# Chunked attention in TensorE's 64x64 tiles, in one section per eight feed-forward units

## Chip, cores, metric

One core of a Trainium2 chip runs the whole kernel. The metric is device time in microseconds (us), the median of several executions. The engines are TensorE (PE, matmuls; PEld is its weight load), VectorE (DVE), ScalarE (ACT), GpSimd (POOL) and SyncE (SP), which issues nearly all DMAs.

## The reference

The first half is a linear attention with decay, over 4 batches, 8 heads, 768 positions and 64 channels; the second is a feed-forward layer on the result, as 3072 tokens of 512 channels.

```python
for b in range(nb):                       # blocks of 64 positions
    qb, kb, vb = (q[:, :, sl], k[:, :, sl], v[:, :, sl])
    intra = np.einsum('bhic,bhjc->bhij', qb, kb) * Dmask[None]
    intra = np.einsum('bhij,bhjd->bhid', intra, vb)
    inter = np.einsum('bhid,bhde->bhie', qb * lam_pow[None], kv_state)
    out[:, :, sl] = intra + inter
    kv_state = lam_block * kv_state + np.einsum('bhsd,bhse->bhde', kb_dec, vb)
...
h = x @ w_in                              # 512 -> 2048
g = h * (1.0 / (1.0 + np.exp(-h)))        # SiLU
return g @ w_out                          # 2048 -> 512
```

## The kernel before

**Tiling.** The 3072 tokens are 24 chunks of 128 positions, six to a batch. A head has 64 channels, so two heads form a pair and the eight heads four pairs (NP). GROUPS (L17) collects chunks into groups of 256 or 384 tokens for the feed-forward layer. All matmul inputs are bf16, all sums fp32.

**Preparation.** The decay is put into q and k: `prep` (L367) multiplies a chunk's q by a table that grows with the position and its k by one that falls, on POOL, to qb and kb. `dma_t` (L382) has two DMA transposes on SP's queue turn them into qt and kn (channels on partitions). `vcast` (L374) rounds v to bf16 on ACT. `next_prep` (L685) does this for the next chunk and issues the loads of a later one.

**Attention of a chunk, from the seventh (c >= 6) on.** TensorE is used whole, as 128x128, so a pair's two heads have to be kept apart by zeros. For that DVE spreads kn into ktbd (`move_k`, L408, 64x512) and v into vpad (`spread_v`, L394, 64x256): block-diagonal buffers whose other halves stay zero. Then come
- the scores (`pe_s`, L484): eight matmuls into two banks sp, four of 128 columns and four of 64, and the causal mask on DVE (`masked`, L494) to ss;
- the state (`pe_d`, L456): four matmuls into kv_ps, accumulated over a batch's chunks in PSUM, and the two diagonal halves copied by DVE into kvbd (`copy_kv`, L468); a batch's last chunk has none;
- the output (`pe_o`, L505): four matmuls of qt with kvbd (not in a batch's first chunk), four of 128 and four of 64 columns with ss, into one bank op, which ACT copies into xt, the feed-forward input (L530).

**Feed-forward.** An "up" unit computes hidden channels of a group: for 256 tokens `ffn1_two` (L553) two blocks of 128 channels in eight matmuls of 256 columns, for 384 tokens `ffn1` (L559) one block in four matmuls of 384. ACT applies Silu to each bank h_ps into g. A "down" unit (`ffn2`, L587) is four of the sixteen matmuls (512 columns) of 128 tokens into a bank o_ps; after the fourth unit DVE copies the bank to ob, and `tick` (L579) has SP store it two units later. The last 128 tokens are split in three (`ffn2_last`, L602).

**PSUM.** Eight banks: att (3), h (2), o (2), kv (1).

**What sets the order.** Each engine runs its queue in the order in which the program issues instructions. Chunks 0 to 3 follow a list written out by hand (ORDER, L25); their scores and outputs are already in 64x64 tiles (`op_s`, L295, and `op_o`, L311). Chunks 4 and 5 are written out below it (L714 to L743). From then on `stretch` (L778) merges lists of units by place: the ups of group g, the attention pieces of group g+1, and the downs of group g-1, evenly over the stretch. A piece is s (scores), d (state) or o (output) of a chunk; the first thing in `piece` (L746) is to prepare chunks up to c+3.

Of the kernel before, what the change touches and what calls it, by code (L numbers as in the profile page):

```python
# [16 lines left out]
GROUPS = [256, 256, 256, 256, 256, 384, 384, 384, 384, 256]  # L17
# [21 lines left out]
def kernel(  # L39
# [73 lines left out]
    for i in range(NKV):  # L113
        vpad.append(const.tile([128, NP, 4, D], BF16, name=f"vpad{i}"))
        ktbd.append(const.tile([128, NP, 2, BLK], BF16, name=f"ktbd{i}"))
        kvbd.append(const.tile([128, NP, BLK], BF16, name=f"kvbd{i}"))
# [73 lines left out]
    mask2 = const.tile([128, BLK], F32)  # L190
    for j in range(2):
        nc.gpsimd.tensor_copy(mask2[64 * j:64 * j + 64, :], mask[0:64, :])

    vhalf = [t.rearrange("s p x d -> s p (x d)").rearrange("s p (h j d) -> s p h j d", h=2, j=2) for t in vpad]
    khalf = [t.rearrange("d p j s -> d p (j s)").rearrange("d p (h j s) -> d p h j s", h=2, j=2) for t in ktbd]

    def clear_halves(*bufs):  # L200
        for i in bufs:
            nc.gpsimd.memset(ktbd[i], 0.0)
            nc.gpsimd.memset(vpad[i], 0.0)

    NBUF = {"att": 3, "h": 2, "o": 2, "kv": 1}
# [71 lines left out]
    def op_t(src, name):  # L277
        def run(c, a, tag):
            tp = psum.tile([128, 2, 2, BLK], BF16, name=name, tag=tag, bufs=NBUF[tag], padded_shape=[128, 4, 2, BLK])
            for r in range(2):  # L280
                for p in range(2):
                    nc.tensor.transpose(tp[:, p, r, :], src[c][:, a, r, 2 * p:2 * p + 2, :], ident)
            cell[name, c, a] = tp
        return run
# [10 lines left out]
    def op_s(c, a, *tags):  # L295
        sps = [psum.tile([128, 2, 2, 2, 64], F32, name="sp", tag=t, bufs=NBUF[t]) for t in tags]
# [14 lines left out]
    def op_o(c, a, *tags):  # L311
        for x, t in enumerate(tags):
            op_[c + x, a] = psum.tile([128, 2, 2, 64], F32, name="op", tag=t, bufs=NBUF[t], padded_shape=[128, NP, 2, 64])
# [47 lines left out]
    def prep_k(c, e="P"):  # L361
        kb = nat.tile([128, NP, 2, D], BF16, tag="kb")
        VG[e].tensor_tensor(kb, rawk.pop(c).rearrange("s (p j) d -> s p j d", j=2), decay(lam_bwd, c % NB),  # L363
                                op=AL.mult)
        natb[c] = (None, kb, vpad[c % NKV] if c < NPAD else nat.tile([128, NP, 2, D], BF16, name="vb", tag="vb", bufs=2))

    def prep(c):  # L367
        qb = nat.tile([128, NP, 2, D], BF16, tag="qb")
        nc.gpsimd.tensor_tensor(qb, rawq.pop(c).rearrange("s (p j) d -> s p j d", j=2), decay(lam_fwd, c % NB),  # L369
                                op=AL.mult)  # L370
        prep_k(c)
        natb[c] = (qb,) + natb[c][1:]

    def vcast(c, e="A"):  # L374
        if c in vraw and c >= NPAD:
            vb = natb[c][2]
            move(e, vb, vraw.pop(c).rearrange("s (p j) d -> s p j d", j=2))
            vnew.add(c)
# [3 lines left out]
    def dma_t(c):  # L382
# [5 lines left out]
        tr[c] = (qt, khalf[c % NKV])  # L388
        knat[c] = kn

    knat = {}
    vnew = set()

    def spread_v(c):  # L394
        if c in vnew:
            vnew.discard(c)
            vb, vh = natb[c][2], vhalf[c % NKV]
            for j in range(2):
                for h in range(2):
                    nc.vector.tensor_copy(vh[64 * j:64 * j + 64, :, h, j, :], vb[64 * h:64 * h + 64, :, j, :])  # L400

    def spread_k(c):
        if c in knat:
            kn = knat.pop(c)
            for j in range(2):
                move_k("D", c, j, kn)

    def move_k(e, c, j, t):  # L408

        rows = slice(64 * j, 64 * j + 64)  # L410
        if c < NPAD:
            move(e, ktbd[c % NKV][rows, :, j, :], t[rows, :, :])
        else:
            move(e, khalf[c % NKV][rows, :, :, j, :], t[rows, :, :].rearrange("d p (h s) -> d p h s", h=2))
# [3 lines left out]
    def pe_tq(c, tag):  # L418
        qb = qpairs.pop(c)
        tp = psum.tile([128, 2, NP, BLK], BF16, name="tq", tag=tag, bufs=NBUF[tag])  # L420
# [5 lines left out]
    def copy_qt(c, tp, e="A"):  # L426
# [4 lines left out]
        tr[c] = (qt, ktbd[c % NKV] if c < NPAD else khalf[c % NKV])  # L431

    def pe_tk(c, tag):
        kb = natb[c][1]
        tp = psum.tile([128, NP, BLK], BF16, name="tk", tag=tag, bufs=NBUF[tag], padded_shape=[128, 2 * NP, BLK])
# [7 lines left out]
    def st_t(c):  # L443
        qb, kb, vb = natb[c]
        tp = psum.tile([128, 2, NP, BLK], BF16, name="tp", tag="att", bufs=3)
        for p in range(NP):
            nc.tensor.transpose(tp[:, 0, p, :], qb[:, p, :, :], ident)
        for p in range(NP):
            nc.tensor.transpose(tp[:, 1, p, :], kb[:, p, :, :], ident)
        qt = nat.tile([128, NP, BLK], BF16, tag="qt")  # L450
        nc.vector.tensor_copy(qt, tp[:, 0, :, :])
        for j in range(2):
            move_k("D", c, j, tp[:, 1, :, :])
        tr[c] = (qt, khalf[c % NKV])

    def pe_d(c):  # L456
# [4 lines left out]
        if blk == 0:  # L461
            kvps[c // NB] = psum.tile([128, NP, BLK], F32, name="kv_ps", tag="kv", bufs=1)
        kv = kvps[c // NB]
        for p in range(NP):
            nc.tensor.matmul(kv[:, p, :], lhsT=kb[:, p, :, :], rhs=vb[:, p, 0:4:3, :] if c < NPAD else vb[:, p, :, :],  # L465
                             start=(blk == 0 and p == 0), stop=True, skip_group_check=True)
# [17 lines left out]
    def pe_s(c, j, tag="att"):  # L484

        qt, kt = tr[c]
        a = 0 if c < NPAD else 64 * j
        sp = psum.tile([128, NP, BLK - a], F32, name="sp", tag=tag, bufs=NBUF[tag], padded_shape=[128, NP, BLK])
        for p in range(NP):
            lhsT = kt[:, p, j, :] if c < NPAD else kt[:, p, j, :, :]  # L490
            nc.tensor.matmul(sp[:, p, :], lhsT=lhsT, rhs=qt[:, p, a:], start=True, stop=True)  # L491
        return sp

    def masked(sp, e="D", m=None):  # L494
        n = sp.shape[-1]
        ss = work.tile([128, 4, n], BF16, name="ss", tag="ss", padded_shape=[128, 4, BLK])
        m = mask if m is None else m
        VG[e].tensor_tensor(ss, sp, m[:, None, :n].to_broadcast([128, 4, n]), op=AL.mult)  # L498
        return ss

    def st_s(c):
        spread_k(c)
        st[c] = [masked(pe_s(c, j), m=mask if c < NPAD else mask2) for j in range(2)]

    def pe_o(c, tag="att"):  # L505
        blk = c % NB
# [3 lines left out]
        g, off = group_of[c]  # L510
        if off == 0:
            xt[g] = xpool.tile([128, KO_IN, GROUPS[g]], BF16, name="xt", tag="xt", padded_shape=[128, KO_IN, 512])
        op = psum.tile([128, NP, BLK], F32, name="op", tag=tag, bufs=NBUF[tag])
        terms = [(kvb[c][:, p, :], qt[:, p, :], op[:, p, :]) for p in range(NP)] if blk > 0 else []
        for j in range(2):
            if c < NPAD:
                terms += [(vb[:, p, 2 * j:2 * j + 2, :], res[j][:, p, :], op[:, p, :]) for p in range(NP)]
            else:
                terms += [(vhalf[c % NKV][:, p, j, :, :], res[j][:, p, :], op[:, p, 64 * j:]) for p in range(NP)]

# [3 lines left out]
        return op  # L524

    def st_o(c):
        spread_v(c)
        op = pe_o(c)
        g, off = group_of[c]
        nc.scalar.activation(xt[g][:, :, off * BLK:(off + 1) * BLK], op, AF.Copy)  # L530
# [6 lines left out]
    def ffn1_open(g, i, tag="h"):  # L537
        hps[g, i] = psum.tile([128, 512], F32, name="h_ps", tag=tag, bufs=2)
# [20 lines left out]
    def ffn1(g, m, part=None, tag="h", kos=range(KO_IN)):  # L559
        n = GROUPS[g]  # L560
        a, z = (0, n) if part is None else (part * n // 2, (part + 1) * n // 2)
        if (g, m) not in hps:
            hps[g, m] = psum.tile([128, 512], F32, name="h_ps", tag=tag, bufs=2)
        hp = hps[g, m]
        tick()
        for ko in kos:
            nc.tensor.matmul(hp[:, a:z], lhsT=w_in_bf[:, ko, m * 128:(m + 1) * 128], rhs=xt[g][:, ko, a:z],  # L567
                             start=(ko == 0 and a == 0), stop=(ko == KO_IN - 1), skip_group_check=True)
        if z == n and kos[-1] == KO_IN - 1:
            gg = gpool.tile([128, n], BF16, name="g", tag="g", padded_shape=[128, 512])  # L570
            nc.scalar.activation(gg, hp[:, :n], AF.Silu)  # L571
            gt[g, m] = gg

# [13 lines left out]
    def ffn2(g, mt, kos, tag="o"):  # L587
        tick()
        if kos[0] == 0:
            ops[g, mt] = psum.tile([128, DM], F32, name="o_ps", tag=tag, bufs=2)  # L590
# [11 lines left out]
    def ffn2_last(g, mt):  # L602

        r0 = gstart[g] + mt * BLK
        for i, (a, z, tag) in enumerate([(0, 256, "o"), (256, 384, "h"), (384, 512, "h")]):
            o = psum.tile([128, 512], F32, name="o_part", tag=tag, bufs=2)
# [21 lines left out]
    def op_u(g, b, h, *tags):  # L628
# [9 lines left out]
        for m, tag in zip(ms, tags):  # L638
            hps["m", m] = psum.tile([128, 512], F32, name="h_ps", tag=tag, bufs=2)
# [42 lines left out]
    fns = {"t": st_t, "d": st_d, "s": st_s, "o": st_o}  # L682
# [23 lines left out]
    for i in range(NKV):  # L706
# [35 lines left out]
    clear_halves(0, 1)  # L742
# [3 lines left out]
    def piece(c, kind):  # L746
        while state["prepped"] <= min(c + 3, NCHUNK - 1):
            next_prep()
        fns[kind](c)
        if kind == "s":  # L750
# [74 lines left out]
```

## Time and profile before

| what | value |
|---|---|
| time of three runs | 213.63, 214.12, 214.44 us; median 214.12 |
| span of the profiled execution, first to last instruction | 211.4 us |
| between this span and the median | 2.7 us |
| granted TensorE clock | 1.00 throughout |
| o_ps matmuls, 128x512 (L593) | 368, busy 91.7 us |
| h_ps matmuls, 128x384 (L567) and 128x256 (L544) | 256 and 288, busy 50.6 and 35.9 us |
| scores (L491), outputs (L522), state (L465) | 160, 228, 64 matmuls |
| Silu of 512 columns on ACT (L549) | 596 ns |
| copy of o_ps to ob on DVE (L597) | 691 ns |
| last matmul ends at | 208.7 us |

The profile is one execution; its span leaves out what lies before the first and after the last instruction, so the table sets it beside the median of the timed runs. In the lists of groups, a line gives source line, engine, operation, names and shapes, count, then busy time, mean ns of one, and the engine's idle time before them with what ended it. The timeline gives start, duration and operation, equal neighbours merged ("x8"). A matmul's duration holds its latency, and the next one starts before it ends; so the time that matmuls take is read from the distance of their starts.

### The profile page before, as it was taken

To read this page: it belongs to the slowest core of one execution; us is meant where nothing else is said; L and a number is where in the kernel's file an instruction comes from. 1 tells how busy PE (TensorE), PEld (TensorE's weight loads), DVE (VectorE), ACT (ScalarE), POOL (GpSimd) and SP (SyncE) were. 2 spreads that over 40 slices of the span, in tenths; PEclk is the share of its full clock that TensorE was granted. 3 is DMA by queue.
4 is the path that set the end of the run, shared out by engine and by line. 5 is a ranking of instruction groups with operands and counts; after the bars stand their busy time and mean duration, and the time that the engine had idled before them with its cause. 6 is when DMAs were issued, how large, how long until landed. Compare 5 with 4: busy or idle time off the path is not lost.

```text
span 211.4 us, 4349 instructions
## 1 busy us (share of the span) xinstructions
PE 204.5 (97%) x1698; PEld 127.5 (60%) x1698; DVE 116.3 (55%) x266; ACT 96.4 (46%) x183; POOL 54.1 (26%) x66
## 2 busy tenths in 40 slices
PE   7899999998999999999999999999999999999994
PEld 2467444566857877765665665556665565466654
DVE  3897458586287897563994686355552351110121
ACT  3686762514724664545454544445534344323210
POOL 6360004463933433341343333330000000000000
PEclk9999999999999999999999999999999999999999
DMA  4999999998979898999998999996111011011112
GB/s 118 337 368 393 394 399 284 287 228 186 269 203 208 168 248 212 201 204 143 229 204 176 233 247 197 225 239 139 50 50 54 0 50 54 0 50 50 53 50 99
DMA packets 95573, 38.57 MB, mean 182 GB/s; under 512 B 80960, under 2 KB 88512, under 8 KB 95552
## 3 DMA queue, kind: packets, MB, share of 16 engines
q1 hardware_dynamic: 92288, 37.50, 69.7%
q10 hardware_dynamic: 3264, 0.79, 1.7%
q8 instruction: 13, 0.21, 0.4%
q14 instruction: 8, 0.07, 0.1%
HBM read 27.27 MB, written 6.29 MB: 159 GB/s over the span
## 4 chain that ended last, share of the span: by engine, by line
PE 75%; DMA 13%; POOL 4%; SPq 3%; ACT 1%; issue 1%; ACTq 1%; DVE 0%; POOLq 0%
PE o_ps L593 32%; PE h_ps L567 18%; DMA qf<-in_q_dram 8%; PE h_ps L544 8%; PE h_ps L644 5%; PE op L522 4%; PE sp L491 3%; DMA kn<-kb 2%; DMA pair<-in_k_dram 2%; SPq L237 2%; POOL qb L369 2%; PE o_part L608 2%; POOL kb L363 2%; PE kv_ps L465 1%; PE kv_ps L343 1%
## 5 line engine op out<-in xcount | busy, mean ns | idle before, releaser
L593 PE MATMUL o_ps<-w_out_bf,g 128*128 128x512 bf16 x368 | 91.7, 379 | 0.0
L593 PEld LDWEIGHTS <-g 128*128 128x128 bf16 x368 | 34.9, 98 | 31.0
L571 ACT ACTIVATE g<-h_ps 128x384 bf16<-128x384 f32 x64 | 31.4, 490 | 47.3 <-PE h_ps L567 46.8
L567 PE MATMUL h_ps<-xt,w_in_bf 128*128 128x384 bf16 x256 | 50.6, 326 | 0.0
L597 DVE COPY ob<-o_ps 128x512 f32<-128x512 f32 x23 | 15.9, 691 | 42.2 <-PE o_ps L593 42.1
L544 PE MATMUL h_ps<-xt,w_in_bf 128*128 128x256 bf16 x288 | 35.9, 273 | 0.9 <-ACT g L549 0.9
L369 POOL TENSOR_TENSOR qb<-qf,lam_fwd 128x512 bf16<-128x512 f32 x18 | 18.8, 1045 | 60.6 <-DMA qf<-in_q_dram 60.6
L567 PEld LDWEIGHTS <-w_in_bf 128*128 128x128 bf16 x256 | 23.7, 98 | 17.2
L549 ACT ACTIVATE g<-h_ps 128x512 bf16<-128x512 f32 x36 | 21.1, 596 | 24.6 <-PE h_ps L544 24.3
L544 PEld LDWEIGHTS <-w_in_bf 128*128 128x128 bf16 x288 | 27.2, 98 | 6.5 <-issue 1.0
L498 DVE TENSOR_TENSOR ss<-sp,mask 128x512 bf16<-128x512 f32 (+1 forms) x40 | 21.0, 566 | 16.7 <-PE sp L491 16.3
L400 DVE COPY vpad<-vb 64x256 bf16<-64x256 bf16 x72 | 23.6, 328 | 2.4 <-ACT vb L184 0.9
L363 POOL TENSOR_TENSOR kb<-kf,lam_bwd 128x512 bf16<-128x512 f32 x20 | 21.7, 1088 | 2.3 <-DMA kf<-in_k_dram 2.1
L188 DVE CAST kvbd<-kv_ps 64x256 bf16<-64x256 f32 x34 | 14.3, 420 | 8.7 <-PE kv_ps L465 8.3
L530 ACT ACTIVATE xt<-op 128x512 bf16<-128x512 f32 x20 | 11.9, 597 | 15.1 <-PE op L522 14.5
L188 DVE COPY ktbd<-kn 64x512 bf16<-64x512 bf16 x36 | 14.5, 402 | 6.5 <-DMA kn<-kb 6.1
L491 PEld LDWEIGHTS <-ktbd 128*128 128x128 bf16 x160 | 9.4, 98 | 4.3 <-DVE ktbd L188 0.9
L184 ACT ACTIVATE vb<-vf 128x512 bf16<-128x512 f32 x18 | 11.2, 622 | 1.7 <-issue 1.7
L491 PE MATMUL sp<-qt,ktbd 128*128 128x128 bf16 (+1 forms) x160 | 10.3, 207 | 0.6 <-DVE ktbd L188 0.6
L644 PE MATMUL h_ps<-xt,w_in_bf 128*128 128x512 bf16 x48 | 10.5, 379 | 0.0
L522 PE MATMUL op<-ss,vpad 128*128 128x128 bf16 (+1 forms) x160 | 10.3, 207 | 0.0
L522 PEld LDWEIGHTS <-vpad 128*128 128x128 bf16 x160 | 8.9, 98 | 0.7
(84 smaller groups left out, 129.9 us busy)
## 6 DMA issues: line engine op xcount, KB each, us to landing
out_dram<-ob SPq DMA_DIRECT2D x23, 256.0 KB, 3.1
kf<-in_k_dram SPq DMA_DIRECT2D x19, 256.0 KB, 3.9
vf<-in_v_dram SPq DMA_DIRECT2D x19, 256.0 KB, 4.3
qf<-in_q_dram SPq DMA_DIRECT2D x17, 256.0 KB, 3.2
pair<-in_moe_w_out_dram SPq DMA_DIRECT2D x8, 512.0 KB, 7.7
pair<-in_moe_w_in_dram SPq DMA_DIRECT2D x6, 512.0 KB, 7.6
pair<-in_k_dram SPq DMA_DIRECT2D x4, 256.0 KB, 4.5
pair<-in_q_dram SPq DMA_DIRECT2D x4, 256.0 KB, 4.6
```

Source lines behind the costliest of these rows:

```text
L188: nc.vector.tensor_copy(dst, src)
L363: VG[e].tensor_tensor(kb, rawk.pop(c).rearrange("s (p j) d -> s p j d", j=2), decay(lam_bwd, c % NB), op=AL.mult)
L369: nc.gpsimd.tensor_tensor(qb, rawq.pop(c).rearrange("s (p j) d -> s p j d", j=2), decay(lam_fwd, c % NB), op=AL.mult)
L400: nc.vector.tensor_copy(vh[64 * j:64 * j + 64, :, h, j, :], vb[64 * h:64 * h + 64, :, j, :])
L491: nc.tensor.matmul(sp[:, p, :], lhsT=lhsT, rhs=qt[:, p, a:], start=True, stop=True)
L522: nc.tensor.matmul(dst, lhsT=lhsT, rhs=rhs, start=(i == 0), stop=(i >= len(terms) - NP), skip_group_check=True)
L544: nc.tensor.matmul(hps[g, i][:, a:a + 256], lhsT=w_in_bf[:, ko, m * 128:(m + 1) * 128], rhs=xt[g][:, ko, :], start=(ko == 0 and u == 0), s ...
L549: nc.scalar.activation(gg.rearrange("p u n -> p (u n)"), hps[g, i], AF.Silu)
L567: nc.tensor.matmul(hp[:, a:z], lhsT=w_in_bf[:, ko, m * 128:(m + 1) * 128], rhs=xt[g][:, ko, a:z], start=(ko == 0 and a == 0), stop=(ko == ...
L571: nc.scalar.activation(gg, hp[:, :n], AF.Silu)
L593: nc.tensor.matmul(o, lhsT=gt[g, ko][:, mt * BLK:(mt + 1) * BLK], rhs=w_out_bf[:, ko, :], start=(ko == 0), stop=(ko == KO_OUT - 1))
L644: nc.tensor.matmul(hps["m", m], lhsT=w_in_bf[:, ko, m * 128:(m + 1) * 128], rhs=xall[0][:, :, ko, :], start=(ko == 0), stop=(ko == KO_IN - 1))
```

## The change

1. **All groups have 256 tokens** (twelve); `ffn1` goes, every up is `ffn1_two`.
2. **No spreading.** From chunk 6 on ktbd and vpad are not filled; two instead of four of each exist, and the four POOL clears (`clear_halves`) go. Matmuls read kn, vb and kvs directly, one head at a time, as 64x64 tiles.
3. **`section(co, cs)`** issues output and state of chunk co and the scores of chunk cs together. It makes a list of matmuls for each of the four tiles (row half r of the inputs, column half x of the result) and merges the lists by an assumed time: 32 ns for 64 columns, 56 for others, always the tile that can begin first. Two row tiles may not write one bank at once. So for each such bank (kv and the two halves of op) one row tile leads; the other's first matmul is preceded by a `nop` that waits for the leader's last matmul (a turn), and the planner places it LAG = 220 ns behind that one's stream. A section has 56 matmuls where co is inside a batch, 48 for a batch's first chunk, 40 for its last, 24 for chunk 23; one more section, of scores alone (chunk 6), has 16.
4. **Behind the matmuls** DVE masks the scores in four products (64x256 twice, 128x256 twice), op is in two banks (two pairs each) and goes to xt in two copies of 128x256, on DVE in the first section of a group and on ACT in the second, and DVE copies the state once (128x256) to kvs.
5. **PSUM.** `bank("o")` takes the o banks in turn; a section takes three att banks and the o bank that the next `ffn2` will open.
6. **Order.** Per group: six ups, a section, two ups, six downs, a section, two downs; the downs are those of the same group. `vcast` stands behind the first and third down.
7. **POOL.** From chunk 6 on each multiplication is split in two, of 384 and 128 elements; the first swaps the two heads of its three pairs (a reversed read).

```diff
-GROUPS = [256, 256, 256, 256, 256, 384, 384, 384, 384, 256]
+GROUPS = [256] * 12
...
+    def bank(tag):
+        if tag != "o":
+            return {"tag": tag, "bufs": NBUF[tag]}
+        otag[0] = 1 - otag[0]
+        return {"tag": f"o{otag[0]}", "bufs": 1}
...
+        nc.gpsimd.tensor_tensor(dst[:, :3], src[:, :3, ::-1, :], by[:, :3, ::-1, :], op=AL.mult)
+        nc.gpsimd.tensor_tensor(dst[:, 3:], src[:, 3:], by[:, 3:], op=AL.mult)
...
+    at = [(1, 0), (1, 0), (1, 0), (0, 1)]
+    LAG = 220
+
+    def section(co=None, cs=None, e="A"):
...
+            ops = [psum.tile([128, 2, BLK], F32, name="op", tag=t, bufs=n, padded_shape=[128, NP, BLK])
+                   for t, n in (("att", 3), (f"o{1 - otag[0]}", 1))]
...
+            sps = [psum.tile([128, NP, BLK], F32, name="sp", tag="att", bufs=3) for j in range(2)]
+
+        def out(r, i):
+            first = {0, 1} if r == i else set()
+            for p in (2 * i, 2 * i + 1):
+                for j in range(2):
+                    x = at[p][j]
+                    add(r, x, i, vb[half[r], p, x, :], res[j][half[r], p, 64 * r:], ops[i][half[x], p % 2, 64 * r:], x in first)
+                    first.discard(x)
+                if blk:
+                    x = at[p][r]
+                    add(r, x, i, kvb[co][half[r], p, :], qt[half[r], p, :], ops[i][half[x], p % 2, :])
+
+        def state(r):
+            if blk < NB - 1:
+                for p in range(NP):
+                    for j in range(2):
+                        add(r, j, "kv", kb[half[r], p, j, :], vb[half[r], p, at[p][j], :], kv[half[j], p, :],
+                            blk == 0 and r == 1 and p == 0)
+
+        def scores(r):
+            if cs is not None:
+                for p in range(NP):
+                    for h in range(2):
+                        add(r, h, "s", kt[half[r], p, half[h]], qs[half[r], p, 64 * h:], sps[r][half[h], p, 64 * h:], True)
+
+        if co is not None:
+            out(0, 0)
+        scores(0)
+        if co is not None:
+            state(0), out(0, 1), state(1), out(1, 1)
+        scores(1)
+        if co is not None:
+            out(1, 0)
+
+        leads = {"kv": 1, 0: 0, 1: 1}
...
+        while any(jobs.values()):
+            k = min((k for k in jobs if jobs[k]), key=lambda k: (begin(k), k))
+            t = begin(k)
+            key, n, lhsT, rhs, dst, start = jobs[k].pop(0)
+            if leads.get(key, k[0]) != k[0] and key in last:
+                turn = nc.tensor.nop()
+                tc.add_manual_dep(turn.ins, last.pop(key).ins.name,
...
+            ins = nc.tensor.matmul(dst, lhsT=lhsT, rhs=rhs, start=start, stop=True, skip_group_check=True)
+            free[k] = t + (32 if n == 64 else 56)
+            if leads.get(key) == k[0]:
+                done[key], last[key] = max(free[k], done.get(key, 0)), ins
...
+            for rows, cols in ((half[0], half[0]), (slice(0, 128), half[1])):
+                m = mask[rows, cols]
+                for ss, sp in zip(st[cs], sps):
+                    nc.vector.tensor_tensor(ss[rows, :, cols], sp[rows, :, cols],
+                                            m[:, None, :].to_broadcast([m.shape[0], NP, 64]), op=AL.mult)
+        if co is not None:
+            x = new_xt(co)
+            for i, op in enumerate(ops):
+                move(e, x[:, 2 * i:2 * i + 2, :], op)
+            if blk < NB - 1:
+                kvs = nat.tile([128, NP, D], BF16, name="kvs", tag="kvs", bufs=2)
+                nc.vector.tensor_copy(kvs, kv)
+                kvb[co + 1] = kvs
...
-    clear_halves(0, 1)
     down0(3, 1)
...
+    def piece(co, cs, e="A"):
+        while state["prepped"] <= min(cs + 2, NCHUNK - 1):
+            next_prep()
+        section(co, cs if cs < NCHUNK else None, e)
...
+    for g in range(2, len(GROUPS) - 1):
+        c = 2 * g + 2
+        for i in range(8):
+            if g == 2 and i == 2:
+                vcast(6)
+                piece(None, 6)
+            if g == 2 and i == 4:
+                next_prep(2)
+            if i == 6:
+                piece(c, c + 1, "D")
+            ffn1_two(g, i)
+        for i, unit in enumerate(downs(g)):
+            if i == 1:
+                vcast(c + 1)
+            if i == 3 and c + 2 < NCHUNK:
+                vcast(c + 2)
+            if i == 6:
+                piece(c + 1, c + 2)
+            ffn2(*unit)
```

## The prediction

> **What bounds the kernel now.** I read the page first (busy shares, then the 40 slices), then the chain of work that ended last, then the waits, then TensorE's timeline.
>
> ```profile
> PE 204.5 (97%) x1698; PEld 127.5 (60%) x1698; DVE 116.3 (55%) x266; ACT 96.4 (46%) x183; POOL 54.1 (26%) x66
> ...
> PE   7899999998999999999999999999999999999994
> ...
> PE 75%; DMA 13%; POOL 4%; SPq 3%; ACT 1%; issue 1%; ACTq 1%; DVE 0%; POOLq 0%
> ```
>
> TensorE (PE) is busy in every slice from 10 us on, and the chain is 75% PE. No other engine is over 55%, so what DVE and POOL lose or gain counts only where PE has to wait for it. The DMA part of the chain lies at 66 to 99 us and ends in small PE waits; I price them below. So time follows the length of PE's stream, matmul by matmul, plus its waits. The timeline prices the stream (start in us, duration, operation; the distance of starts is the price, because matmuls overlap):
>
> ```profile
> 61.26 0.50 PE L491 MATMUL sp<-qt,ktbd 128*128 128x128 bf16 x8
> 61.60 1.03 PE L593 MATMUL o_ps<-w_out_bf,g 128*128 128x512 bf16 x4
> 62.47 0.39 PE L465 MATMUL kv_ps<-vb,kb 128*128 128x128 bf16 x4
> 62.69 1.03 PE L593 MATMUL o_ps<-w_out_bf,g 128*128 128x512 bf16 x4
> 63.55 0.39 PE L522 MATMUL op<-qt,kvbd 128*128 128x128 bf16 x4
> 63.78 0.50 PE L522 MATMUL op<-ss,vpad 128*128 128x128 bf16 x8
> 64.12 1.89 PE L593 MATMUL o_ps<-w_out_bf,g 128*128 128x512 bf16 x8
> ```
>
> Four kv_ps matmuls take 62.69-62.47 = 0.22 us, so 56 ns for 128 columns; the eight sp matmuls (four of 128, four of 64 columns) take 0.34, so 29 ns for 64 columns; o_ps takes 0.865 per four. A chunk's attention is 0.34+0.22+0.23+0.34 = 1.13 us of PE, and nothing but PE's order hides it.
>
> **Removed.** Chunks 6 to 23 issue 264 matmuls of 128 and 144 of 64 columns: 264 x 56 + 144 x 29 ns = 19.0 us (in the trace their starts add up to 18.9). DVE loses the copies into vpad (72, 23.6 us) and ktbd (36, 14.5 us), POOL the four clears: worth nothing by themselves, DVE is covered by PE. But two PE waits for ktbd go with them, and a third for ACT:
>
> ```profile
> 48.91 1.91 PE L544 MATMUL h_ps<-xt,w_in_bf 128*128 128x256 bf16 x16
> 51.67 4.53 PE L544 MATMUL h_ps<-xt,w_in_bf 128*128 128x256 bf16 x40 [0.85 <-ACT g L549]
> ...
> 98.35 1.03 PE L593 MATMUL o_ps<-w_out_bf,g 128*128 128x512 bf16 x4
> 99.82 0.51 PE L491 MATMUL sp<-qt,ktbd 128*128 128x128 bf16 x8 [0.44 <-DVE ktbd L188]
> ```
>
> Sixteen ups at 108 ns end at 50.64, the next starts at 51.67: 1.03 us. Likewise 99.82 - 99.21 = 0.61, and 0.34 at 71.68. The first wait (ACT is issuing three loads) is filled by chunk 6's scores, which the change puts there. The other two come from transposes that arrive late while chunks are taken every 5.3 us; afterwards one is taken every 7.8 us (eight ups, eight downs and two sections, 13.9 + 1.8 us, per two chunks), and loads and transposes run at 5.3 to 5.9 us a chunk here. I take all three: -2.0 us; at worst none.
>
> **Moved at no price.** Ups in 384 columns cost 0.65 us per four, so 163 ns for 384 against 108 for 256: the same per column (41.7 against 41.6 us for those tokens). Downs keep their 368 matmuls. Downs behind their own ups need the last Silu 2.6 us (three downs units) after the last up; it takes 0.6. Eight ups in a row were run at 51.67 without a gap, so ACT's 0.60 per 0.87 us keeps up. Of the copies into xt, those of the second chunk of a group are ACT's: 2 x 0.46 us behind the section, with two downs units (1.73 us) before the ups that read them: hidden with 0.7 to spare. POOL gets two multiplications for one; at 1.05 us per 512 elements its 2.2 us per 7.8 us are far from the bound even if the reversed read doubled them. The transposes, loads and stores on SP's queue are the same in number and order per chunk, and each chunk has more time.
>
> **Added: 19 sections.** The built order has 936 matmuls in 64x64 tiles, 408 of 128 and 528 of 64 columns. The kernel already does this in its first chunks:
>
> ```profile
> 12.33 0.40 PE L282 MATMUL tq<-ident,qb 128*128 128x128 bf16 x4
> 12.56 0.28 PE L318 MATMUL op<-qtp,kvbd 128*128 128x128 bf16 x2
> 12.77 0.42 PE L323 MATMUL op<-ss,vp 64*64 64x128 bf16 x16
> 13.12 0.40 PE L282 MATMUL tk<-ident,kp 128*128 128x128 bf16 x4
> 13.44 0.42 PE L301 MATMUL sp<-qtp,ktp 64*64 64x128 bf16 x16
> ```
>
> Sixteen tile matmuls take 0.35 us, not 16 x 56 = 0.90: four run at once. In the single records four start within 10 ns, and each round of four comes 56 ns after the last one.
> - Stream: (408 x 56 + 528 x 29)/4 ns = **9.5 us** if the four tiles are evenly filled.
> - Mode switches: the first round starts 149 ns after the last L318, not 56, and takes 80, not 56; from the start of the last round to the next L282 it is 159, not 56, and then 66, not 56. That is 93 + 24 + 103 + 10 ns, 0.23 us a visit; 19 x 0.23 = **4.4 us**.
> - Turns: 51 times the second row tile of a bank waits for the first one's last matmul (three per section with output, two without state). No such wait binds in this trace. A 128-column matmul ends 219 ns after its start, 163 after its stream; a semaphore of another engine releases PE within about 50 ns (ACT g to L544 at 51.67). From below 0: the order puts other tiles' work in front, by an assumed 220 ns. From above the whole 163+50+28 (a weight load) = 0.24 each, 12 us. Walking the built order of a full section (56 matmuls) with these prices I get 0.67 us from first to last where even filling gives 0.57: 0.10 x 18 = **1.9 us**, near the lower end, because the 220 ns is close to 0.24.
> - Supply: 56 pairs of load and matmul in under 0.7 us is denser than anything here. From below nothing; from above, 22 pairs were issued within 0.6 us of a late release at 10.98, so at most 27 ns a pair, 25 us for 936, 14 more than stream and turns. The nearest rows, blocks of 16 pairs, show no shortage, so I take 0.
>
> A 64x64 tile's weights load in 28 ns in the single records (second load of a tile after the first), just under the 29 ns of a 64-column matmul, so I count no extra for it.
>
> The Trainium skill speaks against this point: "TensorEngine Tiling (Array Packing)", Restrictions and Gotchas, says that column tiling excludes the fast weight load, and "TensorE: Matmul & The Clock Gate", LDWEIGHTS, gives a load as its columns over 1.2 GHz. By that an estimate of 53 ns per load would set the pace of the 64-column matmuls, 528 x 24/4 ns = 3.2 us more, about 214.8 in all.
>
> **The new wait.** In the section before the last two ups, both halves of op go to DVE, behind the four mask products. The second half's bank is the one that the group's first down takes, and PE's queue stops there: all later matmuls stand behind that first down. The rows:
>
> ```profile
> L498 DVE TENSOR_TENSOR ss<-sp,mask 128x256 bf16<-128x256 f32 x18 | 7.5, 414 | 0.0
> L188 DVE CAST xt<-op 128x256 bf16<-128x256 f32 x2 | 0.9, 441 | 0.0
> ```
>
> Successive mask products start earlier than the last one's end: two (690 and 414 ns) at 62.19 let the next start at 63.13, so 0.94, about 0.33 for each small one. The scores are done shortly before the section's last matmul starts (T); DVE begins near T-0.07, has 4 x 0.33 + 2 x 0.44 = 2.2 us and releases PE at about T+2.18. PE arrives at T + 0.16 (stream and switch) + 1.73 (two ups) = T+1.89. That is 0.29 us, in nine groups **2.6 us**. From below 0 (the masks start 0.3 earlier); from above 0.63 each, 5.7 us (no overlap, 414 each).
>
> **Sum.** -18.9 - 2.0 + 9.5 + 4.4 + 1.9 + 2.6 = -2.5 us. The profiled span is 211.4 us, the median 214.12, so 2.7 us lie around the span; I leave them. Span 208.9, time **211.6 us**.
>
> **Rivals.**
> - *Better: turns and DVE are covered.* Both unknowns at 0: 4.5 us less, 207.1. For it: the 220 ns nearly covers a turn. Against it: 2.2 us of DVE behind 1.9 us of PE.
> - *Break-even.* The gain is what is left of 20.9 us given for 18.4. If the two ktbd waits stay (1.0) and the DVE wait is halfway up (1.5), 214.1.
> - *Slower: turns bind.* PE issues in order, so a turn that is not yet ready holds all four tiles. At the full 0.24 us, 51 turns cost 12.2 instead of 1.9: 221.9. It decides from (1.9+2.5)/51 = 0.086 us a turn (no gain), and 0.107 for slower by 0.5%. For it: no self-wait of PE binds in this trace, so the release time is unseen. Against: the order leaves 220 ns.
> - *Tiles do not run side by side in mixed sizes.* 408 x 56 + 528 x 29 ns = 38.2 instead of 9.5: about 240. Against it: the L323 and L301 rows.
>
> **How the numbers follow.** Forecast (209 to 213) 0.50, better 0.17, break-even 0.15, slower by turns or supply 0.16, no overlap 0.02. A measurement of this kernel can tell about 0.5% (1.07 us) from no change. Faster by more than that: 0.67; within: 0.15; slower: 0.18. The range goes from the better rival, 207.0, up over the DVE bound (211.6 + 3.1) and a third of the way to binding turns (211.6 + 3.4 and more) to 217.0; beyond lie some 0.15 to 0.2.
>
> **What would show it.** A full section should stand in PE's timeline as some 0.9 us from the last up before it to the first after it, not 1.1 (slower) or 0.8 (better). Each group's first down should wait about 0.3 us for DVE's xt copy. No wait for kn or qt at the scores. I am wrong if the gaps inside sections exceed 0.2 us, if 64-column matmuls in one tile stand 50 ns apart, or if the ups wait for xt or ACT.

## The result, and the profile after

| | before | after |
|---|---|---|
| median (lowest to highest), same chip | 213.88 us (213.34 to 214.44) | 211.37 us (210.93 to 212.29) |
| span of the profiled execution | 211.4 us | 209.7 us |
| first up of group 2 starts, last matmul ends | 48.91, 208.67 us | 49.27, 206.95 us |
| between the two (called the **stream** below) | 159.76 us | 157.69 us |

The ratio is 0.9898, with an interval of 0.9863 to 0.9933: faster by about 1%. What lies before 48.9 us is nearly the same work in both kernels, and its length varies by some 0.4 us between executions (48.86 to 49.27 us in three profiles of after), so the comparisons below use the stream, which is taken from one profile of each kernel.

The page of the kernel after, busy shares, two rows of slices and the chain:

```profile
PE 203.4 (97%) x2354; PEld 132.4 (63%) x2354; DVE 83.1 (40%) x193; ACT 89.0 (42%) x167; POOL 54.3 (26%) x96
...
PE   7789999999999999999999999999999999999994
...
PE 91%; SPq 3%; DMA 2%; POOL 1%; issue 1%; DVE 0%; POOLq 0%
```

DVE lost 33 us of work (116.3 to 83.1), and this alone is worth nothing, as PE was the bound and still is. In the chain DMA fell from 13% to 2% and PE rose to 91%: the chain no longer leaves PE at 66 to 99 us for loads and the transposes behind them.

PE's timeline of after around one section (start, duration, operation; neighbours merged):

```profile
65.65 5.40 PE L596 MATMUL h_ps<-xt,w_in_bf 128*128 128x256 bf16 x48
70.98 0.24 PE L563 MATMUL op<-ss,vb 64*64 64x128 bf16 x2
70.99 0.25 PE L563 MATMUL kv_ps<-vb,kb 64*64 64x64 bf16 x4
71.06 0.22 PE L563 MATMUL op<-ss,vb 64*64 64x128 bf16 x1
...
71.38 0.22 PE L563 MATMUL kv_ps<-vb,kb 64*64 64x64 bf16 x2
71.39 0.24 PE L563 MATMUL sp<-qt,kn 64*64 64x128 bf16 x1
71.43 0.22 PE L563 MATMUL kv_ps<-vb,kb 64*64 64x64 bf16 x3
71.47 0.22 PE L563 MATMUL sp<-qt,kn 64*64 64x128 bf16 x1
71.47 0.19 PE L563 MATMUL kv_ps<-vb,kb 64*64 64x64 bf16 x1
...
71.66 0.22 PE L563 MATMUL op<-ss,vb 64*64 64x128 bf16 x1
71.81 1.92 PE L596 MATMUL h_ps<-xt,w_in_bf 128*128 128x256 bf16 x16
73.74 5.35 PE L630 MATMUL o_ps<-w_out_bf,g 128*128 128x512 bf16 x24
```

The 56 matmuls start between 70.98 and 71.66, and the next up starts at 71.81. In single records the section takes 820 ns from its first start to the next up's (820 or 821 in all twelve of this size); with the gap of 93 ns ahead of it and 10 ns behind, 0.92 us. The last two lines show the new wait: sixteen ups at 109 ns end their turn at 71.81 + 1.75 = 73.56, and the first down starts at 73.74. What it waits for stands on DVE's timeline of the same execution (idle time in brackets):

```profile
71.61 1.41 DVE L573 TENSOR_TENSOR ss<-sp,mask 64x256 bf16<-64x256 f32 x4 [5.07 <-PE sp L563]
72.95 0.74 DVE L189 CAST xt<-op 128x256 bf16<-128x256 f32 x2
73.61 0.41 DVE L581 CAST kvs<-kv_ps 128x256 bf16<-128x256 f32 x1
```

The second xt copy ends at 73.68, 0.06 us before the down that takes its bank. Both copies stand behind 1.34 us of masks. The list of waits of after has no wait of PE for a Silu, for ktbd or kn, or for qt in the sections; what is left in them is this (line, releaser, total, times, longest):

```profile
PEld L630 <- DVE xt L189: 1.8, 6, 0.3
```

The list catches six of the nine, and measures from the weight load on; in PE's starts all nine first downs stand 176 to 184 ns late.

### The profile page after: what moved, and what is told of

Same layout as the page of the kernel before. It is cut to its first block, busy times and chain, and to the rows that moved or that the text cites. A ratio compares the mean times of both kernels' runs of the same rounds, so it can differ in the third digit from the quotient of the medians.

```text
span 209.7 us, 5579 instructions
## 1 busy us (share of the span) xinstructions
PE 203.4 (97%) x2354; PEld 132.4 (63%) x2354; DVE 83.1 (40%) x193; ACT 89.0 (42%) x167; POOL 54.3 (26%) x96
## 4 chain that ended last, share of the span: by engine, by line
PE 91%; SPq 3%; DMA 2%; POOL 1%; issue 1%; DVE 0%; POOLq 0%
PE o_ps L630 39%; PE h_ps L596 36%; PE h_ps L681 5%; PE op L563 4%; SPq L231 3%; DMA pair<-in_q_dram 2%; PE sp L563 2%; PE o_part L645 2%; PE kv_ps L563 1%; PE op L478 1%; PE sp L452 1%; POOL vp L260 1%; POOL qb L260 0%; PE kv_ps L337 0%; PE op L317 0%
## 5 line engine op out<-in xcount | busy, mean ns | idle before, releaser
L596 PE MATMUL h_ps<-xt,w_in_bf 128*128 128x256 bf16 x672 | 77.1, 273 | 0.0
L596 PEld LDWEIGHTS <-w_in_bf 128*128 128x128 bf16 x672 | 64.8, 98 | 10.6
L601 ACT ACTIVATE g<-h_ps 128x512 bf16<-128x512 f32 x84 | 49.8, 597 | 48.0 <-PE h_ps L596 47.9
L573 DVE TENSOR_TENSOR ss<-sp,mask 64x256 bf16<-64x256 f32 (+1 forms) x72 | 25.4, 408 | 57.0 <-PE sp L563 57.0
L361 POOL TENSOR_TENSOR qb<-qf,lam_fwd 128x384 bf16<-128x384 f32 x18 | 14.9, 829 | 69.1 <-DMA qf<-in_q_dram 69.1
L361 POOL TENSOR_TENSOR kb<-kf,lam_bwd 128x384 bf16<-128x384 f32 x18 | 14.9, 828 | 10.2 <-issue 4.8
L563 PE MATMUL op<-ss,vb 64*64 64x128 bf16 (+1 forms) x288 | 14.8, 211 | 0.0
L563 PEld LDWEIGHTS <-vb 64*64 64x64 bf16 x288 | 9.6, 106 | 5.8 <-issue 5.7
L563 PE MATMUL op<-qt,kvs 64*64 64x128 bf16 x120 | 10.2, 218 | 0.0
L563 PE MATMUL sp<-qt,kn 64*64 64x128 bf16 (+1 forms) x288 | 9.5, 206 | 0.0
L681 PEld LDWEIGHTS <-w_in_bf 128*128 128x128 bf16 x48 | 4.7, 98 | 5.4
L690 ACT ACTIVATE g<-h_ps 128x512 bf16<-128x512 f32 x12 | 6.5, 595 | 3.4 <-PE h_ps L681 3.4
```

The lines of the kernel that those rows point to most:

```text
L361: nc.gpsimd.tensor_tensor(dst[:, :3], src[:, :3, ::-1, :], by[:, :3, ::-1, :], op=AL.mult)
L563: ins = nc.tensor.matmul(dst, lhsT=lhsT, rhs=rhs, start=start, stop=True, skip_group_check=True)
L573: nc.vector.tensor_tensor(ss[rows, :, cols], sp[rows, :, cols], m[:, None, :].to_broadcast([m.shape[0], NP, 64]), op=AL.mult)
L596: nc.tensor.matmul(hps[g, i][:, a:a + 256], lhsT=w_in_bf[:, ko, m * 128:(m + 1) * 128], rhs=xt[g][:, ko, :], start=(ko == 0 and u == 0), s ...
L601: nc.scalar.activation(gg.rearrange("p u n -> p (u n)"), hps[g, i], AF.Silu)
L681: nc.tensor.matmul(hps["m", m], lhsT=w_in_bf[:, ko, m * 128:(m + 1) * 128], rhs=xall[0][:, :, ko, :], start=(ko == 0), stop=(ko == KO_IN - 1))
```

## Experiments

The first four kernels shared one chip (before: 212.47 us there), the next four a second one (213.45), the last three a third (213.22). Each ratio is against before on the same chip.

**1. The xt copies of the first section on ACT.** This takes away the wait in front of the first downs, by another engine instead of DVE.

```diff
-                piece(c, c + 1, "D")
+                piece(c, c + 1)
```

> Edit: in the changed kernel, the first section of a group also leaves its two copies into xt to ACT, so that they no longer stand behind DVE's masks. Theory (PE is the bound and its queue stops at the group's first down, 0.18 us in each of nine groups in the trace of the changed kernel): the nine waits go, 1.6 us less, 209.8 us against 213.9 before, ratio 0.981. Rival (the wait covers something that is late anyway, as the Silu of the last two ups behind the copies on ACT): no change, 211.4 us, ratio 0.989; then PE waits for ACT at the downs or ups instead.

209.78 us, ratio 0.9873 (0.9849 to 0.9897). The stream is 155.99, 1.70 less than after's 157.69, and no first down waits. Nine waits of 0.18 us are 1.6, so the wait cost what its gaps say and nothing else takes its place.

**2. The new order without the tiles.** Before's functions (128x128 matmuls, spreading, clears) called in the order of after: state, output and scores of a chunk in one piece after six units.

```diff
+    def piece(co, cs):
+        while state["prepped"] <= min(cs + 2, NCHUNK - 1):
...
+        if co is not None:
+            pe_d(co)
+            st_o(co)
+        if cs < NCHUNK:
+            st_s(cs)
+        if co is not None:
+            copy_kv(co)
```

> Edit: the new order alone. Kernel before (whole-array attention with ktbd and vpad, masks as before, xt copied by ACT) with twelve groups of 256, and output, state and scores of two chunks issued together where the changed kernel has its sections. Theory (the sum of the trace: the order takes away 2.0 us of waits for ACT and ktbd; the tiles take 18.9 us of matmuls away and give 16.9 us back, and 1.6 us of the new DVE wait are not in this kernel): 2.0 us less than before, 211.9 us, ratio 0.991, PE idle under 0.5 us after the first up of the third group. Rival (the tiles carry the gain, and in the new order other waits take the place of those three): 213.9 us, ratio 1.00.

219.83 us, ratio 1.0354 (1.0316 to 1.0393). Neither theory holds: the kernel met a wait of its own. Its timelines of PE, of DVE and of POOL, in that order:

```profile
54.43 0.39 PE L465 MATMUL kv_ps<-vb,kb 128*128 128x128 bf16 x4
59.99 0.82 PE L522 MATMUL op<-ss,vpad 128*128 128x128 bf16 x8 [5.17 <-DVE vpad L400]
60.62 0.83 PE L491 MATMUL sp<-qt,ktbd 128*128 128x128 bf16 x8
61.26 3.60 PE L544 MATMUL h_ps<-xt,w_in_bf 128*128 128x256 bf16 x16
64.94 1.24 PE L593 MATMUL o_ps<-w_out_bf,g 128*128 128x512 bf16 x5
```

```profile
54.40 4.08 DVE L188 COPY ktbd<-kn 64x512 bf16<-64x512 bf16 x2 [2.29 <-DMA kn<-kb]
58.50 1.69 DVE L400 COPY vpad<-vb 64x256 bf16<-64x256 bf16 x4
```

```profile
53.67 0.95 POOL L202 MEMSET ktbd<- 128x1024 bf16 x1
54.56 0.95 POOL L203 MEMSET vpad<- 128x1024 bf16 x1
55.45 0.95 POOL L202 MEMSET ktbd<- 128x1024 bf16 x1
56.35 0.95 POOL L203 MEMSET vpad<- 128x1024 bf16 x1
```

The first of the two ktbd copies, 0.29 us at the median of this kernel, takes 3.04 us here and ends 0.14 us after the last clear; the second takes 1.03 us and the first vpad copy 0.97 (0.22 at the median), beside the two multiplications that POOL runs next. The vpad copies that PE's output needs stand behind all this on DVE. PE idles for 5.2 us, then runs slowly: the sixteen ups take 64.94 - 61.26 = 3.68 us, against 1.75 in after, the eight outputs 0.63 instead of 0.34. The wait, the ups and the two attention parts add up to 5.2 + 1.9 + 0.6 = 7.7 us; the time is 7.4 above before's, and the stream, 166.18 us, is 7.7 above that of the mended kernel (experiment 6). So this run says nothing on the order alone, and it was mended in experiment 6.

**3. The group sizes alone.**

```diff
-GROUPS = [256, 256, 256, 256, 256, 384, 384, 384, 384, 256]
+GROUPS = [256] * 12
```

> Edit: kernel before with GROUPS = [256] * 12, and its own merged order otherwise. Theory (ups cost the same per column at 256 as at 384): 213.9 us within 1 us, ratio 0.996 to 1.004; the late transposes may cost more or less, since chunks are taken at another pace. Rival (the group size itself costs or brings something, a Silu of 512 columns for every eight matmuls, or weight loads of 98 ns that no longer hide under 108 ns): over 216 us, PE pitch of the ups above 112 ns.

212.83 us, ratio 1.0007 (0.9989 to 1.0026): no difference. The stream is 159.41, with three small waits left in it (0.70, 0.18 and 0.40 us) where before has 1.03, 0.34 and 0.61. The waits shrank by 0.70, the stream by only 0.35: some 0.35 us is spread over the matmuls of the new shape. Most of it are the ups: in before's starts 256 matmuls of 384 columns take 41.62 us, and 384 of 256 columns, at 109.2 ns each, take 41.92.

**4. Twenty more changes into the tiles.** A 64x64 matmul of zeros with 64 columns, ahead of the third and fifth ups of ten groups, into the bank that the up then overwrites.

```diff
+        if g > 1 and i in (2, 4):
+            nc.tensor.matmul(hps[g, i][0:64, 0:64], lhsT=zero[0:64, :64], rhs=zero[0:64, :64], start=True, stop=True, skip_group_check=True)
```

> Edit: changed kernel with one matmul of zeros more, 64 columns in a 64x64 tile, ahead of the third and the fifth up of the groups 2 to 11, into the bank that the up then overwrites: 20 visits to the tile mode more that do nothing. Theory (a visit costs 0.23 us of switching whatever it holds, and 0.03 for the matmul): 5.2 us more than the changed kernel, 216.6 us, ratio 1.013. Rival (the 0.23 us are the tail of the section and the head of the next matmul, which any change of operands costs): under 2 us more, 213 us.

215.91 us, ratio 1.0159 (1.0141 to 1.0177). PE's timeline of this kernel, at two of the visits:

```profile
67.25 0.21 PE L609 MATMUL h_ps<-zero 64*64 64x64 bf16 x1
67.39 1.92 PE L596 MATMUL h_ps<-xt,w_in_bf 128*128 128x256 bf16 x16
69.24 0.21 PE L609 MATMUL h_ps<-zero 64*64 64x64 bf16 x1
```

From visit to visit it is 1.99 us, where sixteen ups alone take 1.75: 0.24 a visit. The whole stream, 162.42, is 4.73 above after's, 0.237 a visit. The matmul itself is 29 ns of it, so going into the tiles and back costs 0.21 us. The records of a full section of after give about the same: 93 ns ahead, 24 more in the first round, 92 behind the last matmul's stream and 10 in the next operation, 0.22 in sum.

**5. After, again** (no edit), beside the next three.

> Edit: none, the changed kernel beside the next three. Both theories: ratio 0.99 to the kernel before, within 0.986 to 0.993.

211.56 us, ratio 0.9909 (0.9878 to 0.994), stream 157.69, the same to the last digit.

**6. The new order without the tiles, mended.** As experiment 2, but on DVE the copies of v stand ahead of the copies that wait for the next chunk's transposes, and chunks from 6 on have four ktbd and vpad buffers of their own, so that POOL has nothing to clear (g has 26 buffers instead of 33 to make room).

```diff
+    def kvi(c):
+        return c % NKV if c < NPAD else 2 + (c - 6) % 4
...
-    for i in range(NKV):
+    for i in range(6):
...
-    clear_halves(0, 1)
```

> Edit: as order_alone, but the copies of v stand ahead of the copies that wait for the next chunk's transposes on DVE, and chunks from the seventh on have four ktbd and vpad buffers of their own, so that the four clears on POOL are not needed (g has 26 buffers instead of 33 to make room). In order_alone PE stood 5.3 us at the seventh chunk's output: a ktbd copy of 0.28 us had taken 3.04 us on DVE while POOL cleared, with vpad's copies behind it. Theory (order takes 2.0 us of waits away, tiles almost nothing net): 2.0 us less than before, ratio 0.991. Rival (tiles carry the gain, because without them the new order has DVE's copies as waits somewhere): ratio 1.00 or above, with PE waits for ktbd or vpad in the trace.

212.06 us, ratio 0.9932 (0.9899 to 0.9965); stream 158.47, so 1.29 below before and 0.78 above after. PE's timeline at the one wait that is left and at a later chunk:

```profile
55.09 0.50 PE L527 MATMUL op<-ss,vpad 128*128 128x128 bf16 x8
55.75 0.52 PE L496 MATMUL sp<-qt,ktbd 128*128 128x128 bf16 x8 [0.16 <-DVE ktbd L193]
```

```profile
71.12 0.39 PE L470 MATMUL kv_ps<-vb,kb 128*128 128x128 bf16 x4
71.34 0.39 PE L527 MATMUL op<-qt,kvbd 128*128 128x128 bf16 x4
71.57 0.50 PE L527 MATMUL op<-ss,vpad 128*128 128x128 bf16 x8
71.91 0.50 PE L496 MATMUL sp<-qt,ktbd 128*128 128x128 bf16 x8
72.25 1.91 PE L549 MATMUL h_ps<-xt,w_in_bf 128*128 128x256 bf16 x16
```

A chunk's attention takes 72.25 - 71.12 = 1.13 us here and 0.92 in the tiles. Of the 2.07 us that the change gained in the stream, 1.29 come with the order (its groups of 256 tokens included), which needs no tiles, and 0.78 with the tiles. The two time intervals overlap, so this split rests on the two streams. The waits agree with it: the order removes 2.0 - 0.33 us of PE's waits and gives 0.3 back in the ups (experiment 3), and the tiles give 18.9 - 16.85 us (below), take back 1.6 for the new wait and remove the last 0.33, in sum 0.78.

**7 and 8. Turns with no planned lead, and with a longer one.** LAG is how far behind the leader's stream the planner puts the other row tile's first matmul.

```diff
-    LAG = 220
+    LAG = 0
```

> Edit: changed kernel with LAG = 0, so that the planner puts the second row tile's matmul behind its leader at once, and the turn's wait binds. Theory (a binding turn costs about 0.24 us, in order, whatever the other tiles have to do): up to 51 x 0.24 = 12 us less the 0.15 us per section that are idle already (2.7 us), so 5 to 9 us more than the changed kernel; a full section takes 1.1 to 1.4 us from its first matmul to the next up instead of 0.82. Rival (turns cost next to nothing, and the 0.15 us of a section over the even filling come from uneven tiles): under 1 us more.

```diff
-    LAG = 220
+    LAG = 330
```

> Edit: changed kernel with LAG = 330, so that no turn should bind; other tiles' work stands in front where there is any. Theory (at 220 the turns are nearly covered; what is left of the 0.15 us is uneven filling): a full section stays at 0.82 us within 0.05, time within 0.7 us of the changed kernel. Rival (the turns still bind at 220 by some 50 ns each): sections 0.1 us shorter, 1.8 us less.

LAG 0: 212.19 us, ratio 0.9936 (0.9903 to 0.9968), stream 158.66, 0.97 more than after. I had expected 5 to 9 us more; that failed. A full section is only 49 ns longer (870 against 821), those with 48 matmuls 40 to 77, those with 40 matmuls 91, and the one of chunk 23, which has 24 and nothing beside its turns, 217. PE's timeline of chunk 23's section in this kernel, and its line in the list of waits:

```profile
191.06 0.50 PE L563 MATMUL op<-ss,vb 64*64 64x64 bf16 x3
191.32 0.24 PE L563 MATMUL op<-qt,kvs 64*64 64x128 bf16 x1
191.40 0.44 PE L563 MATMUL op<-ss,vb 64*64 64x128 bf16 x4
191.63 0.27 PE L563 MATMUL op<-qt,kvs 64*64 64x128 bf16 x3
```

```profile
PEld L563 <- PE op L563: 0.4, 2, 0.2
```

Here the wait of PE for PE itself can be seen, twice: gaps of 240 and 222 ns between starts, where a 128-column matmul alone makes 56, so 184 and 166 more. A turn that binds fully costs 0.17 to 0.18 us. But in a full section LAG = 0 does not take the lead away, because the tiles' lists themselves put the scores between leader and follower: in the section at 70.96, 21 matmuls start between the last kv_ps of the leading row tile and the first of the other, 269 ns apart, where after has 270. So this run doesn't show what it costs when all 51 turns bind.

LAG 330: 211.0 us, ratio 0.9895 (0.9841 to 0.9949), stream 157.58. A full section takes 817 or 818 ns, 3 less than with 220, so a longer lead buys nothing there. Chunk 23's section, which has nothing else to issue, keeps one gap of 184 ns between starts at 220 and at 330.

**9. After, a third time** (no edit), beside the last two.

> Edit: none, the changed kernel beside the next two. Ratio 0.99 to the kernel before, within 0.986 to 0.994.

211.03 us, ratio 0.9908 (0.9886 to 0.9931), stream 157.67.

**10. The xt copies ahead of the masks, still on DVE.** This tells whether experiment 1 gained by the engine or by the place in the queue.

```diff
+        if co is not None:
+            x = new_xt(co)
+            for i, op in enumerate(ops):
+                move(e, x[:, 2 * i:2 * i + 2, :], op)
...
-            x = new_xt(co)
-            for i, op in enumerate(ops):
-                move(e, x[:, 2 * i:2 * i + 2, :], op)
```

> Edit: changed kernel with the copies into xt ahead of the four mask products on DVE (they stay on DVE in a group's first section). Theory (the wait at the first down is the place of these copies behind 1.3 us of masks, not the engine that makes them): the first down no longer waits, PE's stream from the third group's first up to the end is 1.6 to 1.7 us shorter, as in xt_on_act (156.0 us against 157.7), and the masks come 0.66 us later at no price, since their reader is five units away. Rival (DVE as such is too slow for this bank, or the later masks are missed at the next section): no gain, 157.7 us, with PE waiting for ss or xt.

209.28 us, ratio 0.9833 (0.9808 to 0.9858), stream 156.06. DVE's and then PE's timeline of this kernel at the section shown above:

```profile
71.26 0.76 DVE L189 CAST xt<-op 128x256 bf16<-128x256 f32 x2 [5.47 <-PE op L563]
71.93 1.40 DVE L577 TENSOR_TENSOR ss<-sp,mask 64x256 bf16<-64x256 f32 x4
```

```profile
71.05 1.92 PE L597 MATMUL h_ps<-xt,w_in_bf 128*128 128x256 bf16 x16
72.81 1.89 PE L631 MATMUL o_ps<-w_out_bf,g 128*128 128x512 bf16 x8
```

The copies end at 72.02, and the first down starts 1.76 us after the first of the sixteen ups: no wait. The masks now end at 73.33, and nothing waits for that: the outputs that read them come six downs later. It was the place in the queue; four lines moved up bring all that the other engine brought.

**11. Both: xt on ACT and LAG 330.**

> Edit: changed kernel with all copies into xt on ACT and LAG = 330. Theory: the two edits touch different waits and add up: 1.7 us from the copies and 0.1 us of PE's stream from the longer lag (157.7 to 157.6 us in the runs with one of them), so 155.9 us from the third group's first up, ratio 0.982 to the kernel before, 0.991 to the changed kernel. Rival (the shorter stream runs into the Silu of the last two ups, which stand behind the copies on ACT): 156.5 us or more, with PE waiting for g or h_ps.

209.32 us, ratio 0.9832 (0.9807 to 0.9857), stream 155.93. It beats before by 1.7% and after, on the same chip, by 209.32/211.03 = 0.992. It can't be told from experiment 10.

## Why the prediction came out right, point by point

The forecast was 211.6 us and the change by -2.5; measured were 211.37 and -2.5. Two of its terms were mis-sized by about 1.0 us each, with opposite signs, so the agreement to 0.2 us is partly luck.

| step | forecast, us | measured, us | from |
|---|---|---|---|
| attention matmuls removed | -18.9 | -18.9 | starts in the trace of before |
| three PE waits gone | -2.0 | -2.0 | 1.96 in before's starts; 0.07 of the first is left in after, counted in the next row |
| the 19 sections (9.5 + 4.4 + 1.9) | +15.8 | +16.85 | first start to the next operation's start, 14.89 in all, and 19 x 0.103 |
| supply of instructions | 0 | 0 | 56 pairs of load and matmul in 0.67 us |
| DVE's wait before the first down | +2.6 | +1.6 | nine gaps of 0.18; experiments 1 and 10 |
| sum | -2.5 | -2.45 | stream: -2.07 |

- **The sections' last term was too small.** The 1.9 us, "Turns", should be 16.85 - 9.5 - 4.4 = 2.95. The step that failed is "0.10 x 18": one full section was walked, and its excess over even filling was taken for all. From single records, less even filling and 0.23 us of switching, a full section leaves 0.13 us, the three of 48 matmuls (779 ns from first start to the next operation's) 0.20 each, the two of 40 (765 ns) 0.19, chunk 23's (760 ns) 0.35 and the scores alone (413 ns) 0.12. So the twelve full ones are 0.2 us over their share of the forecast and the seven short ones 0.8. By the sum of its matmuls at 56 and 29 ns, the fullest tile of a section of 48 or of chunk 23's has 0.11 us more than even filling, that of a full one 0.06.
- **What fills a full section is known in part.** The walk gave 0.67 us, first matmul to last one's end of stream; measured are 672 + 56 = 728 ns. The fullest tile has 624 ns and the emptiest 404, where even filling is 568. So of the 160 ns over even filling 56 are the fullest tile and 24 the first round's slower start; the other 80 no run took apart. LAG 330 takes off 3 ns, so it isn't a short lead, but that doesn't clear the turns. The section of scores alone, the only one without a turn, takes 198 + 56 = 254 ns, just 6 more than its fullest tile (224) and the 24. And right behind the first turn of a full section the matmuls have the first round's durations again (213 and 240 ns instead of 193 and 216), with the next kv_ps of a tile 52 ns later instead of 32.
- **Mode switches held.** 0.23 us a visit was read off one pair of places in the first chunks. Added visits cost 0.21 (experiment 4).
- **DVE's wait was in the right place, and its size was off.** The masks went at the pitch forecast (71.61 to 72.95 for four, 0.33 each). The step that failed is "2 x 0.44" for the two xt copies: they overlap as the masks do, 0.74 us together. That and small shifts make 0.18 instead of 0.29 us.
- **The three waits went** because of the order, as said: with the tiles left out (experiment 6) all but 0.33 us of them went as well. The first went only in part as forecast. ACT's timeline of before has the rounding of v in front of the group's first Silus:

```profile
50.51 0.63 ACT L184 ACTIVATE vb<-vf 128x512 bf16<-128x512 f32 x1 [1.67 <-issue]
51.04 1.06 ACT L549 ACTIVATE g<-h_ps 128x512 bf16<-128x512 f32 x2
```

These Silus start 2.13 us after the group's first up (48.91). In after they start at 50.87, 1.60 us after it (49.27), and the rounding follows at 51.84, since `vcast(6)` now stands behind two ups. That is worth about half of the 1.03 us; chunk 6's scores, 0.45 us with their switch, fill the rest but for 0.07.

- **Moved at no price held.** In the sections and behind them PE waits for xt in front of the first down, and never for a transpose; the up behind chunk 6's scores starts 0.07 us late. POOL's split multiplications take 829 ns for 384 elements, and its busy time is 54.3 us after 54.1.
- **The rest.** Stream and sum differ by 0.4 us. Of that 0.3 are the ups, which the forecast took as equal per column (41.7 against 41.6 us): their starts give 41.9, and experiment 3 agrees (0.35).
- **Rivals.** "Slower: turns bind" needed 0.107 us a turn in all 51 to make the kernel slower by 0.5%. A turn that bound fully cost 0.17 to 0.18, so its price was near the rival's 0.24; but few bound fully, because the order keeps other tiles' matmuls in between, even at LAG 0. "Better" did not come, as DVE's wait was there; an edit that takes this wait out gives 209.3, not 207.1, since the sections' last term stays.
- **The rule on weight loads.** The rule cited from the Trainium skill ("TensorEngine Tiling (Array Packing)", Restrictions and Gotchas, with "TensorE: Matmul & The Clock Gate", LDWEIGHTS), by which 64-column matmuls would keep to an estimated 53 ns, isn't borne out. In after's timeline above, the last eight kv_ps matmuls, four in each of two tiles, start from 71.38 on, within 0.12 us, and in single records, taken in their order of issue, those of one tile stand 52, 32 and 31 or 32 ns apart: only the first pair, behind a turn, is near 53. The measurement decides. The prediction's own argument, a load "in 28 ns", is misread, though: 28 ns is the distance between the starts of two loads, and in the records these loads last 102 to 107 ns each.

## What to carry to other kernels

Before you change the form of a stage, try its order alone: here 1.29 of the 2.07 us came with the new order, and could have been had with the old matmuls. Small tiles that run side by side pay a fixed price for every visit (0.21 us here), and a section can't be shorter than its fullest tile (624 ns here, where even filling is 568); so collect work into few visits and fill the tiles evenly. If you price one kind of section, price the others too: here the short ones held most of the error. And where a bank goes straight on to the next matmuls, put its evacuation first in the evacuating engine's queue: that one move was worth 1.6 us, most of what the whole change had gained.

## What the runs showed of the hardware that was not expected

- **SBUF copies on DVE stretch while POOL writes or reads.** In experiment 2 a 64x512 copy took 3.04 us during four clears on POOL, against 0.29 at the median. In experiment 6, with no clears, four vpad copies took 2.63 us at 52.45, beside two multiplications of POOL, against 4 x 0.22. DVE's products and casts out of PSUM keep their 402 to 419 ns in after. The Trainium skill ("SBUF — State Buffer", Who interferes with whom) says that DVE's two-port copies and a GpSimd instruction lock each other out of a shared port, the later one until the earlier is done; these runs agree in kind, but the copy was held over several POOL instructions and not over one. No run here moved POOL's work away from an otherwise unchanged copy.
- **A wait of some 5 us on PE costs more than the wait.** In experiment 2 the granted clock is 0.8 in the slice of the wait and 0.5 in the next, and the sixteen ups there took 1.9 us more. The waits of up to 1.03 us in before left it at 1.00. The row of granted clocks of experiment 2's kernel, in tenths:

```profile
PEclk9999999999859999999999999999999999999999
```

- **A turn of TensorE on itself costs 0.17 to 0.18 us when nothing else is left to issue.** That was seen in chunk 23's section at LAG 0. In a full section, with 270 ns between the leader's last kv_ps and the follower's first, filled by other tiles' matmuls, 110 ns more of planned lead took off only 3 ns.
